# Second expert's first matrix product as seven block products, and its PReLU as a·h + |b·h|

## The chip, the cores and the metric

One core of a Trainium2 chip runs the kernel. The metric is the device time of one execution in microseconds (us); the median of three runs is compared. Engines are named as in the profile: PE (TensorE) with its weight loads PEld, DVE (VectorE), ACT (ScalarE), POOL (GpSimd), SP (which issues the transfers).

## The reference, cut to what matters

```python
X = fft(fft(x, axis=1), axis=2).real        # x: 2 x 3008 x 256, float32
x = X.reshape(6016, 256)
h = x @ w_in;  g = h / (1 + exp(-h));  x = g @ w_out          # first expert, 256 -> 2048 -> 256
h = x @ w_in2; g = max(h, 0) + alpha * min(h, 0); return g @ w_out2   # second expert (PReLU)
```

`alpha` is one number for each of the 2048 columns of `h`, between 0 and 0.3. The weights come as float64.

## The kernel before, in words

The transform uses the symmetry of real input: rows come in pairs, `NC` = 6 chunks of `CW` = 502 pairs. It runs as three short stages of matrix products (lines up to 371), the second batch's part of it beside the first expert. The first expert then has 96 rounds, one for each chunk and each of the 16 tiles `f` of 128 hidden columns; a scheduler orders these rounds and the work put beside them (`PLAN` gives the rounds), among it the conversion of the second expert's weights from float64 (`conv_w2`) and their splitting.

Everything is computed in float32r (a float32 that the writer rounds to fewer bits), with each operand as a high part and a low part: a product x·w is hi·hi + lo·hi + hi·lo, three matrix products. `split` makes the parts: ACT copies the value to float32r (high), and DVE or POOL subtracts that from the value (low).

The second expert is written out by hand, in program order (`manual_schedule`). Its 12 token tiles `t` (chunk and sign) hold 502 tokens each, transposed: 256 inputs as two blocks of 128 partitions. A round `i` is one token tile and one `f`, 192 in all:

- `h_mm`: six matrix products of 502 columns into one bank of PSUM, `ph` (lines 585 to 587: two input blocks by three products).
- `prelu_split` and `low2`: DVE takes `m` = min(ph, 0)·alpha (line 593), then max(ph, 0) + m (line 597); ACT copies to the high part `gh` (line 601); DVE subtracts for the low part `gl` (line 609).
- `mm4`, two rounds later (`LAG`): six products of 502 columns with `w_out2` into two banks, `a` (line 628), summed over the 16 `f` of a token tile. At the last `f` ACT copies both out (`ot`) and SP sends them off.

The next token tile's high and low parts (`os`) are made by `split_o1` in two pieces, ACT for the high part and POOL for the low one, at rounds 6 and 9 of the 16.

The pools that matter: `big` (ten 8 KB buffers, for inputs, raw weights, chunks `o1` and `os`), `wk` (sixteen buffers of 504 columns), PSUM `mm` (four banks, for `ph`) and `acc` (four banks, for `a`).

## Time and profile before

| | |
|---|---|
| median of 3 runs | 1012.55 us (1012.48 to 1012.71) |
| span of the profiled execution | 1009.7 us; the runs have 2.85 us around a span of that length |
| first expert's rounds | from about 36 to 477 us of the span |
| second expert's rounds | from about 471 to 1005 us |
| busy, whole span | PE 98%, PEld 80%, DVE 77%, ACT 44%, POOL 31% |

The times of matrix products are to be read with care: they are pipelined, so that the mean duration of one (about 0.39 us at 502 columns) is longer than the step from the start of one to the start of the next, and it is the step that a stream of them costs.

### The profile page before, as it was taken

Reading aid. Unit: us, or ns where it says so; the run is one execution under the profiler, and the core shown is the slowest. Engines: PE = TensorE matmul, PEld = TensorE weight load, DVE = VectorE, ACT = ScalarE, POOL = GpSimd, SP = SyncE. Lnnn points to the kernel's source line nnn. Section 1 sums busy time; section 2 is a strip of 40 time slices with the busy share of each in tenths; the row PEclk is TensorE's granted clock in tenths of the full one; section 3 lists DMA queues with packets and bytes.
Section 4 is the critical chain, followed back from the end, with each engine's and each line's share of the span. In section 5 each row is a group of like instructions: output and inputs, shape, how many; then the busy total and the mean of one; then the engine's idle time right before and its main releaser. Section 6 shows DMA issues by size and latency. Waiting matters only on the chain.

```text
span 1009.7 us, 11772 instructions
## 1 busy us (share of the span) xinstructions
PE 986.5 (98%) x4306; PEld 808.3 (80%) x4306; DVE 773.4 (77%) x1132; ACT 440.4 (44%) x776; POOL 311.0 (31%) x255
## 2 busy tenths in 40 slices
PE   7899899999999999999999999999999999999998
PEld 5677687888888788788888888888888888888886
DVE  7898799676786977978877777777767777777765
ACT  3567566564765566676422222232222223222221
POOL 3377869333355565764500000000000000000000
PEclk9799899999999999999999999999999999999999
DMA  8721100220101112000000000000000000000000
GB/s 272 242 94 43 63 22 1 63 89 1 42 1 43 57 43 84 1 18 25 0 21 1 21 1 21 1 21 20 1 21 1 21 1 21 21 0 21 1 21 21
DMA packets 16602, 36.90 MB, mean 37 GB/s; under 512 B 1824, under 2 KB 11296, under 8 KB 14880
## 3 DMA queue, kind: packets, MB, share of 16 engines
q1 hardware_dynamic: 16544, 36.15, 10.8%
q8 instruction: 34, 0.56, 0.2%
q14 instruction: 24, 0.20, 0.1%
HBM read 26.83 MB, written 9.31 MB: 36 GB/s over the span
## 4 chain that ended last, share of the span: by engine, by line
PE 88%; DVE 6%; issue 2%; DMA 1%; ACT 1%; POOL 1%; SPq 0%; DVEq 0%; ACTq 0%
PE a L628 26%; PE ph L586 9%; PE ph L587 9%; PE ph L585 9%; PE a L553 7%; PE a L555 7%; PE a L551 7%; PE pe L505 2%; PE pe L507 2%; PE pe L506 2%; PE po L505 2%; PE po L507 2%; PE po L506 2%; PE psb L318 1%; PE psa L274 1%
## 5 line engine op out<-in xcount | busy, mean ns | idle before, releaser
L601 ACT ACTIVATE gh<-m 128x502 fp32r<-128x502 f32 x192 | 120.0, 625 | 379.2 <-DVE m L597 353.6
L628 PE MATMUL a<-gh,wo 128*128 128x502 f32 x768 | 268.4, 391 | 0.0
L593 DVE TENSOR_SCALAR m<-ph,sm 128x502 f32<-128x502 f32 x192 | 142.1, 740 | 135.9 <-PE ph L587 135.4
L628 PEld LDWEIGHTS a<-gh,wo 128*128 128x128 f32 x768 | 144.6, 188 | 30.4
L533 POOL TENSOR_TENSOR gl<-t,gh 128x502 fp32r<-128x502 f32 x96 | 131.8, 1373 | 100.2 <-ACT t L521 78.8
L160 POOL TENSOR_TENSOR os<-o,os 128x502 fp32r<-128x502 f32 x24 | 29.3, 1222 | 415.8 <-ACT os L159 415.8
L609 DVE TENSOR_TENSOR gl<-m,gh 128x502 fp32r<-128x502 f32 x192 | 150.1, 782 | 1.4 <-ACT gh L601 0.4
L553 PE MATMUL a<-gl,wo 128*128 128x502 f32 x384 | 149.5, 397 | 1.1 <-POOL gl L533 1.0
L586 PE MATMUL ph<-os,wi 128*128 128x502 f32 x384 | 150.2, 391 | 0.0
L585 PE MATMUL ph<-os,wi 128*128 128x502 f32 x384 | 149.8, 390 | 0.0
L628 PE MATMUL a<-gl,wo 128*128 128x502 f32 x384 | 149.6, 390 | 0.0
L587 PE MATMUL ph<-os,wi 128*128 128x502 f32 x384 | 149.6, 389 | 0.0
L555 PE MATMUL a<-gh,wo 128*128 128x502 f32 x384 | 148.1, 394 | 0.0
L597 DVE SCALAR_TENSOR_TENSOR m<-ph,m 128x502 f32<-128x502 f32 x192 | 129.3, 673 | 0.1
L551 PE MATMUL a<-gh,wo 128*128 128x502 f32 x384 | 123.3, 396 | 5.8 <-ACT gh L520 5.8
L520 ACT ACTIVATE gh<-hp 128x502 fp32r<-128x502 f32 x96 | 59.8, 623 | 109.0 <-DVE hp L516 106.8
L513 DVE SCALAR_TENSOR_TENSOR t<-n,sm,pe 128x502 f32<-128x502 f32 x96 | 70.2, 731 | 27.3 <-PE pe L507 25.8
L551 PEld LDWEIGHTS a<-gh,wo 128*128 128x128 f32 x384 | 72.3, 191 | 22.9 <-ACT gh L520 8.3
L553 PEld LDWEIGHTS a<-gl,wo 128*128 128x128 f32 x384 | 73.3, 191 | 18.6 <-POOL gl L533 3.9
L533 POOL TENSOR_TENSOR gl<-hp,gh 128x502 fp32r<-128x502 f32 x52 | 68.5, 1318 | 60.2 <-ACT hp L521 55.1
L555 PEld LDWEIGHTS a<-gh,wo 128*128 128x128 f32 x384 | 73.2, 191 | 15.0
L587 PEld LDWEIGHTS ph<-os,wi 128*128 128x128 f32 x384 | 73.1, 190 | 15.0
(129 smaller groups left out, 1378.2 us busy)
## 6 DMA issues: line engine op xcount, KB each, us to landing
out_t<-ot SPq DMA_DIRECT2D x24, 251.0 KB, 2.5
x<-in_xs SPq DMA_DIRECT2D x8, 512.0 KB, 5.2
raw_i<-in_wi SPq DMA_DIRECT2D x8, 512.0 KB, 5.2
raw_w<-in_wi SPq DMA_DIRECT2D x4, 1024.0 KB, 5.2
raw_w<-in_wo SPq DMA_DIRECT2D x4, 1024.0 KB, 4.8
raw_o<-in_wo SPq DMA_DIRECT2D x3, 1024.0 KB, 6.5
y<-ys SPq DMA_DIRECT2D x16, 144.0 KB, 3.2
x<-in_xs SPq DMA_DIRECT2D x2, 1024.0 KB, 4.9
```

Of the source, the lines that this page charges most:

```text
L533: (nc.gpsimd if s or lo_pool(i + 1) else nc.vector).tensor_tensor(lo, h, hi.bitcast(F32), op=ALU.subtract)
L551: nc.tensor.matmul(ACC1[lb, s], hi, G[i, s][0], start=st, stop=False)
L553: nc.tensor.matmul(ACC1[lb, s], hi, G[i, s][1], start=False, stop=False)
L555: nc.tensor.matmul(ACC1[lb, s], lo, G[i, s][0], start=False, stop=sp)
L585: nc.tensor.matmul(ph, hi, OS[t][:, 2 * k, :], start=k == 0, stop=False)
L586: nc.tensor.matmul(ph, hi, OS[t][:, 2 * k + 1, :], start=False, stop=False)
L587: nc.tensor.matmul(ph, lo, OS[t][:, 2 * k, :], start=False, stop=k == 1)
L593: nc.vector.tensor_scalar(m, ph, 0.0, alpha_sb[:, f : f + 1], op0=ALU.min, op1=ALU.mult)
L597: nc.vector.scalar_tensor_tensor(m, ph, 0.0, m, op0=ALU.max, op1=ALU.add)
L601: nc.scalar.activation(hi, m, AF.Copy)
L609: nc.vector.tensor_tensor(lo, m, hi.bitcast(F32), op=ALU.subtract)
L628: nc.tensor.matmul(ACC2[lb], w[lb][j], x, start=st and first, stop=sp and last)
```

## The change: what it does

The product of the 256-row weight block with a token tile is written as a 2 by 2 block product: the two input blocks of 128 rows, and two tiles of `f` (`4g + k` and `4(g+1) + k`, so one round now holds a pair), on the weights' side; the input blocks and two halves of the tokens on the other. The halves are `L` and `R`, columns 0 to 251 and 250 to 501 (`HALF` = 252; two columns are computed twice). Eight block products become seven, on sums and differences of blocks of the weights (`prep_ws`, made once: `ws0`, `ws1`) and of the tokens (`split_o1`, made for each token tile: `xt`, then `os`). The blocks of `h` are sums of the seven products, some of which accumulate in PSUM, while others are added by DVE.

A round is now a pair of `f`: 96 rounds `n`, eight for each token tile. In a round, `outer` issues products 1 and 5 into the two halves of a bank `ac`, and ACT copies both out (`e`); `inner` issues product 2 into a bank `b`, and products 6 and 3 on top of the halves of `ac`; ACT copies the first half out (`u`); `seventh` issues product 7 on top of that half, and ACT copies it again (`u`, second half); `fourth`, in the next round, issues product 4 on top of it. DVE makes the four blocks of `h`: `h11` (`b` + `e`), `h12` (`ac` + `u`), `h22` (`u` + `e`), and the last is `ac` itself. Each of the 21 matrix products has 252 columns.

PReLU becomes a·h + |b·h|: ACT takes |b·h| (`absolute`, `q`), DVE multiplies and adds (`prelu`). The coefficients a and b come from `alpha` (`coefficients`, on POOL); their sign is moved into `w_out2`, whose rows ACT multiplies before they are split (`prep_wo2`). `mm4` is as before, six products of 502 columns for each `f`, and two rounds of pairs behind.

The new weights lie in buffers that are free by then (`WS_HOMES`), and three new ones (`xs`). `os` now takes two of the `big` buffers for each token tile.

```diff
-    "wi0": (84, 86), "wo0": (86, 87), "wi1": (88, 90), "wo1": (90, 92), "wi2": (98, 100), "wo2": (100, 102),
-    "wi3": (102, 104), "wo3": (104, 106),
+    "co": (60, 61), "ws0": (62, 80), "ws0b": (84, 92), "ws1": (80, 92), "ws1b": (93, 99),
+    "wo0": (86, 87), "wo1": (90, 91), "wo2": (97, 98), "wo3": (98, 100),
 }
+HALF = 252
+WS_ENG = "vpvpvpvpvpv" "pvpvppppppp"
...
+        A11, A12, A21, A22 = (0, 0), (0, 1), (1, 0), (1, 1)
+        steps = put_(4, *A22) + put_(1, *A11)
+        steps += form(A22, A21, A22, ALU.add) + form(A21, A11, A21, ALU.subtract)
+        steps += put_(2, *A12) + put_(5, *A22)
+        steps += form(A11, A22, A11, ALU.subtract) + put_(7, *A21)
+        steps += form(A12, A12, A11, ALU.subtract) + put_(6, *A11) + put_(3, *A12)
...
+            for q in range(2):
+                f = 4 * g + 2 * h + q
+                w = v[:, 256 * q : 256 * q + 256]
+                nc.scalar.activation(w, w, AF.Copy, scale=fc[:, 2, f : f + 1])
...
+            to, p, q = (
+                (t1, b(0, 1), b(0, 0)), (t3, b(1, 1), b(0, 1)), (t2, b(1, 1), t1), (t4, b(1, 0), t2),
+            )[n]
+            nc.gpsimd.tensor_tensor(to, p, q, op=ALU.subtract)
...
+            nc.scalar.activation(hi, src, AF.Copy)
+            nc.gpsimd.tensor_tensor(lo, src, hi.bitcast(F32), op=ALU.subtract)
...
+        for q, (w, x) in enumerate(((whi, xhi), (whi, xlo), (wlo, xhi))):
+            nc.tensor.matmul(to, w, x, start=start and q == 0, stop=q == 2, skip_group_check=True)
...
+        product(n, 1, h["ac"][:, :HALF], True)
+        product(n, 5, h["ac"][:, HALF:], False)
+        h["e"] = work(F32, f"e{n}", 2 * HALF)
+        nc.scalar.activation(h["e"], h["ac"], AF.Copy)
...
+        product(n, 2, h["b"], True)
+        product(n, 6, h["ac"][:, :HALF], False)
+        product(n, 3, h["ac"][:, HALF:], False)
...
+        nc.vector.tensor_tensor(h["h0"][:, :W], h["b"][:, :W], h["e"][:, :W], op=ALU.add)
...
+        nc.scalar.activation(h["u"][:, :HALF], h["ac"][:, :HALF], AF.Copy)
+        nc.vector.tensor_tensor(h["h0"][:, R], h["ac"][:, HALF:], h["u"][:, :HALF], op=ALU.add)
...
+        product(n, 7, h["ac"][:, :HALF], False)
+        nc.scalar.activation(h["u"][:, HALF:], h["ac"][:, :HALF], AF.Copy)
...
+        nc.vector.tensor_tensor(h["h1"][:, R], h["u"][:, HALF:], h["e"][:, HALF:], op=ALU.add)
...
+        product(n, 4, H[n]["ac"][:, :HALF], False)
...
+        nc.scalar.activation(h["q", i][:, to], source(n, part), AF.Abs, scale=coef(n, i, 1))
...
+        nc.vector.scalar_tensor_tensor(
+            h[f"h{i}"][:, to], source(n, part), coef(n, i, 0), h["q", i][:, to], op0=ALU.mult, op1=ALU.add
+        )
...
+                if t + 1 < 2 * NC and 3 <= p < 7:
+                    if p == 3:
+                        nxt = split_o1(t + 1)
+                    run(nxt[(0, 4, 6, 7)[p - 3] : (4, 6, 7, 9)[p - 3]])
...
+                if new:
+                    outer(n)
+                if old:
+                    prelu(n - 1, 0)
+                    h22(n - 1)
+                if n > 1:
+                    low2(n - 2, 1)
+                if old:
+                    absolute(n - 1, 1)
+                    high2(n - 1, 0)
+                if n < 2:
+                    mm2(n1 - LAG + n, (0,))
                 else:
-                    mm4(i - LAG)
+                    mm4(n - 2, 0)
+                if old:
+                    prelu(n - 1, 1)
+                    fourth(n - 1)
+                    absolute(n - 1, 2)
+                if new:
+                    inner(n)
+                    h11(n)
+                if old:
+                    prelu(n - 1, 2)
+                if new:
+                    h12(n)
+                if old:
+                    high2(n - 1, 1)
+                if new:
+                    absolute(n, 0)
+                if old:
+                    low2(n - 1, 0)
...
+                    mm4(n - 2, 1)
+                if new:
+                    seventh(n)
```

How this stands in the engines' queues, at three places. The first is PE in the middle of the second expert. Before, one round of one `f` (`ph` the hidden tile, `a_6_0` and `a_6_1` the two sums of a token tile):

```order
L585 MATMUL ph_6507<-os_6214,wi_1_0_4114 128x502
L586 MATMUL ph_6507<-os_6214,wi_1_0_4114 128x502
L587 MATMUL ph_6507<-os_6214,wi_1_1_4115 128x502
L585 MATMUL ph_6507<-os_6214,wi_1_2_4116 128x502
L586 MATMUL ph_6507<-os_6214,wi_1_2_4116 128x502
L587 MATMUL ph_6507<-os_6214,wi_1_3_4117 128x502
L628 MATMUL a_6_0_6479<-gh_98_6477,wo_0_0_4036 128x502
L628 MATMUL a_6_0_6479<-gl_98_6496,wo_0_0_4036 128x502
L628 MATMUL a_6_0_6479<-gh_98_6477,wo_0_1_4037 128x502
L628 MATMUL a_6_1_6480<-gh_98_6477,wo_0_0_4036 128x502
L628 MATMUL a_6_1_6480<-gl_98_6496,wo_0_0_4036 128x502
L628 MATMUL a_6_1_6480<-gh_98_6477,wo_0_1_4037 128x502
```

Now, from product 3 of a round (`ws_3h`) over the six products of `mm4` to product 7 (`ws_7h`):

```order
L671 MATMUL ac_7423<-os_0_6775,ws_3h 128x252
L671 MATMUL ac_7423<-os_1_6776,ws_3h 128x252
L671 MATMUL ac_7423<-os_0_6775,ws_3l 128x252
L769 MATMUL a_5_0_7177<-gh_44_1_7403,wo_3_0_4579 128x502
L769 MATMUL a_5_0_7177<-gl_44_1_7435,wo_3_0_4579 128x502
L769 MATMUL a_5_0_7177<-gh_44_1_7403,wo_3_1_4580 128x502
L769 MATMUL a_5_1_7178<-gh_44_1_7403,wo_3_0_4579 128x502
L769 MATMUL a_5_1_7178<-gl_44_1_7435,wo_3_0_4579 128x502
L769 MATMUL a_5_1_7178<-gh_44_1_7403,wo_3_1_4580 128x502
L671 MATMUL ac_7423<-os_0_6775,ws_7h 128x252
L671 MATMUL ac_7423<-os_1_6776,ws_7h 128x252
L671 MATMUL ac_7423<-os_0_6775,ws_7l 128x252
```

Between products that write the same bank `ac`, and that wait for ACT and DVE to have read it, stand the six products of an older `f`.

The second place is ACT in the same stretch. Before, it has one copy for each `f` (`gh2`):

```order
L601 ACTIVATE gh2_90_6311<-m90_6306 128x502
L601 ACTIVATE gh2_91_6331<-m91_6326 128x502
L601 ACTIVATE gh2_92_6351<-m92_6346 128x502
L601 ACTIVATE gh2_93_6371<-m93_6366 128x502
L601 ACTIVATE gh2_94_6391<-m94_6386 128x502
```

Now, the last part of the token tile's splitting (`os3`), and one round (the number behind a name is the round):

```order
L656 ACTIVATE os3_0_5747<-xt3_1_5681 128x504
L687 ACTIVATE e22_5888<-ac22_5881 128x504
L733 ACTIVATE q1_21_5895<-h1_21_5891,fc_86 128x252
L744 ACTIVATE gh2_21_0_5897<-h0_21_5856 128x502
L733 ACTIVATE q1_21_5895<-ac21_5816,fc_86 128x250
L705 ACTIVATE u22_5920<-ac22_5881 128x252
L744 ACTIVATE gh2_21_1_5926<-h1_21_5891 128x502
L733 ACTIVATE q0_22_5928<-h0_22_5921,fc_86 128x502
L711 ACTIVATE u22_5920<-ac22_5881 128x252
```

Two copies for a pair of `f` have become eight operations, in a fixed order in which those that PE waits for (`e`, `u`) stand behind the others.

The third place is ACT at the start of the second expert. Before (`wi2`, `wo2`: high parts of the later weights):

```order
L601 ACTIVATE gh2_2_4457<-m2_4452 128x502
L159 ACTIVATE wi2_2_2_4441<-v2_1_2666 128x512
L601 ACTIVATE gh2_3_4481<-m3_4476 128x502
L159 ACTIVATE wo2_2_0_4489<-v2_3_3715 128x512
L601 ACTIVATE gh2_4_4505<-m4_4500 128x502
L159 ACTIVATE wo2_2_0_4489<-v2_3_3715 128x512
```

Now, between the last `u` of round 0 and `e` of round 1:

```order
L711 ACTIVATE u0_4483<-ac0_4458 128x252
L513 ACTIVATE ws1_3h_4501<-v2w_1_3331 128x512
L541 ACTIVATE v2o_1_3739<-v2o_1_3739,fc_86 128x256 x2
L166 ACTIVATE wo2_2_0_4504<-v2o_1_3739 128x512
L541 ACTIVATE v2o_1_3739<-v2o_1_3739,fc_86 128x256 x2
L166 ACTIVATE wo2_2_0_4504<-v2o_1_3739 128x512
L687 ACTIVATE e1_4521<-ac1_4514 128x504
```

Seven operations on weights stand in a row there, ahead of a copy that PE's next products wait for; before, one stood between two copies.

## Rows read from the trace of the kernel before

**Rows 1.** The page: span; busy us by engine (share, instructions); last chain's shares.

```profile
span 1009.7 us, 11772 instructions
PE 986.5 (98%) x4306; PEld 808.3 (80%) x4306; DVE 773.4 (77%) x1132; ACT 440.4 (44%) x776; POOL 311.0 (31%) x255
PE 88%; DVE 6%; issue 2%; DMA 1%; ACT 1%; POOL 1%; SPq 0%; DVEq 0%; ACTq 0%
```

**Rows 2.** 780 to 1000 us: busy PE, PEld, DVE, ACT, POOL (xcount); granted clock; DMA.

```profile
780.00:1000.00 220.00, 220.00 (x965) 181.88 (x964) 161.45 (x242) 58.90 (x98) 9.38 (x8) 1.00 0.03 12
```

**Rows 3.** The page's groups: busy us, mean ns of one, idle before and releaser.

```profile
L601 ACT ACTIVATE gh<-m 128x502 fp32r<-128x502 f32 x192 | 120.0, 625 | 379.2 <-DVE m L597 353.6
L628 PE MATMUL a<-gh,wo 128*128 128x502 f32 x768 | 268.4, 391 | 0.0
L593 DVE TENSOR_SCALAR m<-ph,sm 128x502 f32<-128x502 f32 x192 | 142.1, 740 | 135.9 <-PE ph L587 135.4
```

**Rows 4.** Timeline of one round of the second expert: start us, duration us.

```profile
700.72 0.39 PE L585 MATMUL ph<-os,wi 128*128 128x502 f32 x1
...
701.87 0.40 PE L587 MATMUL ph<-os,wi 128*128 128x502 f32 x1
...
702.30 0.74 DVE L593 TENSOR_SCALAR m<-ph,sm 128x502 f32<-128x502 f32 x1 [0.83 <-PE ph L587]
...
703.46 0.38 PE L585 MATMUL ph<-os,wi 128*128 128x502 f32 x1
```

**Rows 5.** Timeline of three products of 256 columns in the first expert, with loads.

```profile
192.03 0.40 PE L274 MATMUL psa<-xr,fh 128*128 128x256 f32 x2
192.15 0.19 PEld L274 LDWEIGHTS psa<-xr,fl 128*128 128x128 f32 x1
...
192.27 0.19 PEld L505 LDWEIGHTS pe<-eo,wi 128*128 128x128 f32 x1
192.38 0.39 PE L505 MATMUL pe<-eo,wi 128*128 128x502 f32 x1
```

**Rows 6.** ACT's groups by form, from PSUM, from SBUF, and the copy out.

```profile
L156 ACT ACTIVATE ot<-a 128x502 f32<-128x502 f32 x23 | 12.2, 579 | 1.9 <-PE a L628 1.9
...
L156 ACT ACTIVATE ya<-psa 128x256 f32<-128x256 f32 x8 | 3.1, 385 | 1.7 <-PE psa L274 1.3
...
L159 ACT ACTIVATE xr<-x 128x256 fp32r<-128x256 f32 x4 | 1.4, 405 | 3.0 <-POOL xr L160 3.0
```

**Rows 7.** DVE's groups by form: half-width operations, PSUM source and SBUF sources.

```profile
L338 DVE TENSOR_TENSOR z<-psb,z 128x283 fp32r<-128x283 f32 x4 | 1.8, 455 | 5.4 <-ACT z L336 5.4
...
L252 DVE TENSOR_TENSOR x<-x 128x256 f32<-128x256 f32 x2 | 0.8, 425 | 0.1
```

**Rows 8.** POOL's groups by form: a half-width difference, and a very small copy.

```profile
L252 POOL TENSOR_TENSOR x<-x 128x256 f32<-128x256 f32 x2 | 1.5, 740 | 0.0
L254 POOL COPY slot<-x 128x4 f32<-128x4 f32 x4 | 1.6, 405 | 0.1
```

**Rows 9.** Timeline: POOL and DVE make low parts; `gl`: ns min/median/max.

```profile
537.71 0.61 ACT L159 ACTIVATE os<-o 128x502 fp32r<-128x502 f32 x1
...
538.39 1.27 POOL L160 TENSOR_TENSOR os<-o,os 128x502 fp32r<-128x502 f32 x1 [32.79 <-ACT os L159]
538.53 1.67 DVE L609 TENSOR_TENSOR gl<-m,gh 128x502 fp32r<-128x502 f32 x1
...
L609 DVE TENSOR_TENSOR gl<-m,gh x192: 670/673/1798, 479.5 to 1003.2; 128x502 fp32r<-128x502 f32 x192
```

**Rows 10.** Busy time by engine, sum over 300 to 480 us (first expert's second half).

```profile
sum 180.00, PE 177.73 PEld 144.89 DVE 139.66 ACT 113.13 POOL 108.18; mean PE 19.75 PEld 16.10 DVE 15.52 ACT 12.57 POOL 12.02
```

**Rows 11.** The transfer of `alpha` (issue, time to landing), and POOL's first low part.

```profile
31.62 0.43 SPq L700 DMA_DIRECT2D sm<-in_alpha  x1
...
40.22 1.25 POOL L533 TENSOR_TENSOR gl<-hp,gh 128x502 fp32r<-128x502 f32 x1 [0.77 <-ACT hp L521]
...
DMA to landing us min/median/max: 6.1/6.1/6.1
```

More of the change, by code (lines that the diff above doesn't have):

```diff
@@ new lines, in slab, with prep_ws, put_, high @@
+    def slab(home, name):
+        if home in ("cs", "ch"):
+            return wp.tile([128, 512], F32R, tag=home, name=name)
+        if home == "cv":
+            return cp.tile([128, 512], F32R, tag="cv", name=name)
+        if home == "xs":
+            return xp.tile([128, 512], F32R, tag="xs", name=name)
+        if home == "e128":
+            return ep.tile([128, 512], F32R, tag="e128", name=name)
+        return wp.tile([128, 512], F32R, tag=home, name=name)
+    def prep_ws(pg):
+        at = lambda i, k: V2["w", pg][:, 1024 * k + 512 * i : 1024 * k + 512 * i + 512]
+        eng = iter([nc.vector if e == "v" else nc.gpsimd for e in WS_ENG[11 * pg : 11 * pg + 11]])
+        homes = list(WS_HOMES[pg])
+        def put_(j, i, k):
+            def high():
+                hi = slab(homes.pop(0), f"ws{pg}_{j}h")
+                lo = slab(homes.pop(0), f"ws{pg}_{j}l")
+                WS[pg, j] = hi, lo
+                nc.scalar.activation(hi, at(i, k), AF.Copy)
+            def low():
+                hi, lo = WS[pg, j]
+                next(eng).tensor_tensor(lo, at(i, k), hi.bitcast(F32), op=ALU.subtract)
+            return [high, low]
+        def form(to, x, y, op):
+            return [lambda: next(eng).tensor_tensor(at(*to), at(*x), at(*y), op=op)]
+        A11, A12, A21, A22 = (0, 0), (0, 1), (1, 0), (1, 1)
[4 more added lines that the diff above has]
+        steps += form(A12, A12, A11, ALU.subtract) + put_(6, *A11) + put_(3, *A12)
+        return steps
@@ L540, in mm2 @@
         sp = f == NF - 1 or ORDER[i + 1][0] != c
-        if st:
+        if st and 0 in lbs:
             for lb in range(2):
@@ L544, in mm2 @@
                     ACC1[lb, s] = acc_ps(f"a1_{i}_{lb}{s}")
-        more = c in O1
-        if sp and not more:
+        if sp and 0 in lbs:
+            MORE[0] = c in O1
+        more = MORE[0]
+        if sp and not more and 0 in lbs:
             O1[c] = big([128, 4, CW], F32, f"o1_{c}")
-        for lb in range(2):
+        for lb in lbs:
             hi, lo = (WO[1, g, j][:, fo, lb * 128 : lb * 128 + 128] for j in range(2))
@@ L564, in mm2 @@
                         nc.scalar.activation(o, ACC1[lb, s], AF.Copy)
[L565 removed]
+        if 1 in lbs:
+            del G[i, 0], G[i, 1]
     OS = {}
     ACC2 = {}
[L571 to L588 removed]
@@ new lines, in fourth, with source, absolute @@
+    def fourth(n):
+        product(n, 4, H[n]["ac"][:, :HALF], False)
+    PART = {0: (0, slice(0, CW)), 1: (1, R), 2: (1, slice(0, W))}
+    def source(n, part):
+        i, to = PART[part]
+        return H[n]["ac"][:, :W] if part == 2 else H[n][f"h{i}"][:, to]
+    def absolute(n, part):
+        i, to = PART[part]
+        h = H[n]
+        if ("q", i) not in h:
+            h["q", i] = work(F32, f"q{i}_{n}")
+        nc.scalar.activation(h["q", i][:, to], source(n, part), AF.Abs, scale=coef(n, i, 1))
@@ new lines, in prelu, with high2, low2 @@
+    def prelu(n, part):
+        i, to = PART[part]
+        h = H[n]
+        nc.vector.scalar_tensor_tensor(
+            h[f"h{i}"][:, to], source(n, part), coef(n, i, 0), h["q", i][:, to], op0=ALU.mult, op1=ALU.add
+        )
+    def high2(n, i):
+        hi = work(F32R, f"gh2_{n}_{i}")
+        nc.scalar.activation(hi, H[n][f"h{i}"], AF.Copy)
+        G[n, i] = [hi]
+    def low2(n, i):
+        lo = work(F32R, f"gl2_{n}_{i}")
+        nc.vector.tensor_tensor(lo, H[n][f"h{i}"], G[n, i][0].bitcast(F32), op=ALU.subtract)
+        G[n, i].append(lo)
@@ L624, in mm4 @@
             order = [(lb, j, ghi) for lb in range(2) for j in range(2)] + [(lb, 0, glo) for lb in range(2)]
-        for n, (lb, j, x) in enumerate(order):
-            first = all(o[0] != lb for o in order[:n])
-            last = all(o[0] != lb for o in order[n + 1 :])
+        for m, (lb, j, x) in enumerate(order):
+            first = all(o[0] != lb for o in order[:m])
+            last = all(o[0] != lb for o in order[m + 1 :])
             nc.tensor.matmul(ACC2[lb], w[lb][j], x, start=st and first, stop=sp and last)
@@ L754, in fft_moe_kernel @@
             put(a + (b - a) * n // 8, a + (b - a) * (n + 1) // 8, steps)
+        put(*PLAN["co"], [coefficients])
+        for pg in range(2):
+            steps = prep_ws(pg)
+            put(*PLAN[f"ws{pg}"], steps[:8])
+            put(*PLAN[f"ws{pg}b"], steps[8:])
         for g in range(4):
-            put(*PLAN[f"wi{g}"], prep_wi2(g))
             put(*PLAN[f"wo{g}"], prep_wo2(g))
-        put(n1 - 5, n1 - 1, [lambda lb=lb: split_o1(0, lb) for lb in range(2)])
+        put(n1 - 5, n1 - 1, split_o1(0))
         for i in range(n1):
```

165 lines of the change are left out of this document (90 added, 75 removed).

## The prediction

> **What bounds the kernel now.** I read the page first: PE is busy 98% of the span, and 88% of the chain that ended last is PE [rows 1]. An average can hide a stage with another limit, so next came the busy time by stretch. In the second expert PE has no gap at all, 220.00 of 220.00 us at granted clock 1.00, while DVE works 161.45, ACT 58.90 and POOL 9.38 us [rows 2]. The groups say the same from the other side: ACT's copies `gh` sat idle 379.2 us, 353.6 of it until DVE's `m`, and DVE 135.4 us until the last product of `ph` [rows 3]. There the time is the count of matrix products times their step. The timeline gives that step: a round's first `ph` product starts at 700.72, the next round's at 703.46, twelve products later, so 2.74/12 = 0.228 us for 502 columns [rows 4]. A pair of `f` costs 5.48 us, and 96 pairs 526 us.
>
> **The products.** A pair goes from 24 products of 502 columns to 12 of 502 and 21 of 252. No float32r product of 252 columns is in the trace. The nearest have 256: two start from 192.03, one follows, and the next stream starts at 192.38, so a step of 0.35/3 = 0.117 us, give or take 0.003 for times shown to 0.01 us [rows 5]. In proportion to 502 columns it would be 0.1146. I take 0.116, with 0.1146 and 0.120 as bounds. A round then costs 21 x 0.116 + 12 x 0.228 = 5.18 us, 0.30 less, and 96 of them 29 us less (32 and 21 by the bounds).
>
> Each product loads its own weights, 0.19 us by the record, longer than such a step. The row says that this is latency: the loads at 192.15 and 192.27 start 0.12 us apart, under the running products [rows 5]. The Trainium skill ("TensorE: Matmul & The Clock Gate", section "Part 3: Packing small matmuls") speaks against the change here: it says that a load overlaps with products in flight only where the row groups differ, and all of these use all rows. With that page's load of 128/1.2 = 107 ns and stream of N/2.4 + 2.5 ns, an estimate is 0.21 us for a short product and 0.32 for a long one: a round of 8.3 us against 7.7 before, and the products would cost 64 us more instead of 29 less. The trace disagrees, since 0.228 leaves no room for such a load.
>
> **DVE and ACT in a round.** Half-width DVE operations cost 0.455 us at 283 columns from PSUM and 0.425 at 256 from SBUF [rows 7], so about 0.42 at 252. DVE has five of them (`h11`, `h12`, `h22`, two parts of `prelu`), one `prelu` at 502 columns (0.70, between the 0.67 of `gl` and the 0.74 of `m` [rows 3, 9]) and two low parts (0.67): 4.15 us of 5.18, about as much as before for a pair. ACT goes from two copies to eight operations: `e` 0.58, two `u` 0.385, two half `q` 0.385 and 0.405, one `q` and two high parts at 0.625 [rows 3, 6]: 4.0 us. |b·h| with a column of coefficients is priced as a copy; at most a tenth more, 0.1 us a round, still fits. So PE stays the longest by over a microsecond, if nothing waits in the wrong order.
>
> **The new waits.** Products 6, 7 and 4 write a bank that ACT and DVE have to have read. The shortest cover is that of product 7: it waits for `h12`, which waits for `u`, which waits for product 3. PE's result is ready 0.43 us after the start of a product of 502 columns, so 0.20 after its slot [rows 4]; then `u` 0.385, `h12` 0.42, and two handovers of about 0.07 (ACT's `os` ends at 538.32, POOL starts at 538.39 [rows 9]): 1.15 us. The six products of `mm4` between cover 6 x 0.228 = 1.37. The other two have about 2 us of cover for 1 to 1.3 us of work. So in an undisturbed round nothing shows, but only 0.2 us is spare at product 7, with ACT and DVE strictly in order behind it. If ACT reaches `u` late, what is late next is `h12`, product 7, and all of PE.
>
> **What disturbs the rounds.** Once in eight rounds ACT also makes the next token tile's high parts (three of 0.405, two of 0.62) and two copies out (0.58): 3.6 us against 1.1 us free in each round; two of them stand together in one round, just ahead of `e`. POOL's work in a block of eight rounds grows from two differences of 1.27 us to four forms, three half-width lows (0.74 each [rows 8]) and two lows of 504 columns: 7.7 us. POOL's work is not free for DVE: at 538.39 POOL works 1.27 us, and DVE's `gl`, begun at 538.53, takes 1.67 us, 1.0 more than the median of 0.67 and until 0.5 after POOL's end [rows 9]. Before, PE noticed nothing, as DVE had 0.8 us to spare in each round of 2.74 [rows 4]. Now DVE has 1.0 us in each of 5.18. The operations that read PSUM have one source in SBUF, so some POOL work falls beside them. I take 0.4 us lost for each of eleven such blocks, together 5 us; the bounds are 0 and 14, the latter 1.3 us a block.
>
> **The start of the second expert.** ACT now has `ws1_3h` (0.62), four scalings of 256 columns (0.405) and two splits (0.62) in a row ahead of `e` of round 1: 3.5 us [rows 3, 6]. The cover of `e` is 1.3 us up to product 6, so some 2 us reach PE; two later rounds take 1.4 us more of ACT each, and six POOL lows of 512 columns hold DVE up. I take 5 us, bounds 1 and 9. Before, one split at a time stood between two copies, and PE did not wait.
>
> **The first expert.** Added there or at its end: on POOL ten more operations of about 1.3 us, on ACT six high parts and half of the 16 scalings, on DVE four operations of 0.7 us. From 300 to 480 us POOL is busy 108 of 180 us, ACT 113, DVE 140 [rows 10], so most of it finds room. The scheduler also moves `coefficients`, planned for round 60, to just ahead of POOL's first low part. `alpha`, issued at 31.62, lands 6.1 us later, in time, but six small operations (0.25 to 0.4 us, by the 0.405 of a copy of 4 columns [rows 8]) meet 0.77 us of idle POOL [rows 11]: 1 us late. With other small shifts of the scheduler's order I take 2 us, bounds -2 and 6. At the end the work after the last `h` product is much the same: 0.
>
> **Sum.** -29 + 5 + 5 + 2 = -17 us. The profiled execution's span is 1009.7 us, 2.85 us less than the median of the runs shown; I subtract from both alike: span about 993, time 996 us.
>
> **The rivals.**
> - *The chain at product 7 binds in every round.* 0.2 us spare is little, and `u` stands behind a `q` that itself waits for product 4. For it: eight operations on ACT with five waits. Against it: 1.1 us of free ACT time in a round. At 0.15 us a round it costs 14 in place of 5: 1006 us.
> - *DVE, held by POOL, becomes the bound: slower.* Place: the rounds with the lows of `xt`, where POOL's 2.5 us meet DVE's SBUF operations. If half of POOL's 7.7 us a block reaches PE, 11 x 3.85 = 42 us are lost in place of 5: 1034 us. It decides from 0.23 us of waiting a round (22 us in all) on. Against it: 8 us of free DVE time in a block. The Trainium skill ("SBUF — State Buffer", section "SBUF: two separate sides") calls this an exclusive lock, held for the whole instruction; rows 9 agree.
> - *Loads don't hide in a long stream of short products: slower.* If each of the 21 took the 0.19 us of its load, a round would cost 6.7 us and the kernel 1012.6 + 120 = 1132 us. The row with three such products shows no sign, but it is only three. The skill's rule on loads, above, is the same mechanism.
> - *No loss at all.* Only the products count: 1012.6 - 29 to 32, so 981 to 984 us.
> - *It doesn't do what it says* in time: waits of 0.23 us a round give back all: 1012 us.
>
> **How the numbers follow.** Forecast with its small losses (987 to 1003 us) 0.55; no loss 0.11; chain at product 7 (1003 to 1010) 0.13; all given back 0.06; DVE held by POOL 0.11; loads 0.04. The likeliest is 996 us, its own range 987 to 1003. From 983 to 1013 us I leave out the two slower cases, 0.15, and a part of the best one, 0.05. A measurement of this kernel can tell about 0.2%, 2 us: faster 0.79, same 0.06, slower 0.15.
>
> **What would show it.** Steps of 0.116 us within a run of short products, with loads as far apart; rounds of 5.2 us between the starts of product 1; PE's idle time in the second expert below 15 us, and what there is before products 6 or 7, in one or two rounds of eight and in the first four; ACT and DVE each near 80% busy; low parts of 1.5 us and more wherever POOL works. I am wrong if the steps are 0.15 us or more, if PE waits in every round, or if the first expert's rounds have moved by more than 6 us.

## The result, and the profile after

The changed kernel takes 994.09 us (median of 991.82, 993.93, 994.25 and 994.53), the kernel before 1012.51 us beside it: a ratio of 0.9817, 95% interval 0.9803 to 0.9831. The profiled execution took 993.93 us with a span of 992.2 us, 17.5 us less than the 1009.7 of [rows 1].

The page after (span; busy us by engine; shares of the chain that ended last; four groups, to be read as [rows 3]):

```profile
span 992.2 us, 14364 instructions
...
PE 961.0 (97%) x5170; PEld 826.1 (83%) x5170; DVE 789.3 (80%) x1328; ACT 711.2 (72%) x1410; POOL 405.3 (41%) x355
...
PE 79%; DVE 8%; issue 4%; ACT 3%; POOL 3%; DMA 2%; SPq 0%; ACTq 0%; DVEq 0%; POOLq 0%
...
L738 DVE SCALAR_TENSOR_TENSOR h<-h,fc,q 128x502 f32<-128x502 f32 x192 | 130.3, 678 | 38.8 <-ACT q L733 36.7
...
L749 DVE TENSOR_TENSOR gl<-h,gh 128x502 fp32r<-128x502 f32 x192 | 140.6, 732 | 0.1
...
L744 ACT ACTIVATE gh<-h 128x502 fp32r<-128x502 f32 x192 | 118.4, 617 | 2.1 <-DVE h L738 2.1
...
L705 ACT ACTIVATE u<-ac 128x252 f32<-128x252 f32 x96 | 36.6, 381 | 51.7 <-PE ac L671 51.7
```

PE still stands on nearly all of the span. ACT is no longer the idle engine that [rows 3] showed (`gh` had 379.2 us of idle time ahead of it): in the second expert its largest idle time is now 51.7 us, that of the 96 copies `u`, which wait for product 3.

The same views by stretch: the middle of the second expert (answers to [rows 2]), and the first expert's second half (answers to [rows 10]):

```profile
680.00:960.00 280.00, 280.00 (x1785) 254.09 (x1785) 225.32 (x434) 228.54 (x479) 58.03 (x56) 1.00 0.04 14
...
300.00:480.00 180.00, 174.39 (x765) 141.91 (x764) 139.05 (x196) 119.61 (x216) 125.12 (x101) 0.99 0.09 32
```

In the second expert PE again has no gap, now with DVE and ACT busy 80% and 82%. The first expert is where PE stands still more than before: 5.6 us of 180 in place of 2.3.

The timeline of one round (start, duration; answers to [rows 4, 5]):

```profile
700.75 0.42 DVE L706 TENSOR_TENSOR h<-ac,u 128x252 f32<-128x252 f32 x1 [0.30 <-ACT u L705]
...
701.28 0.41 PEld L671 LDWEIGHTS ac<-os,ws_7h 128*128 128x128 f32 x2
...
701.50 0.40 PE L671 MATMUL ac<-os,ws_7h 128*128 128x252 f32 x2
701.62 0.19 PEld L671 LDWEIGHTS ac<-os,ws_7l 128*128 128x128 f32 x1
701.73 0.27 PE L671 MATMUL ac<-os,ws_7l 128*128 128x252 f32 x1
...
702.54 0.39 PE L769 MATMUL a<-gh,wo 128*128 128x502 f32 x1
...
706.66 0.40 PE L671 MATMUL ac<-os,ws_7h 128*128 128x252 f32 x2
```

Nine short products run from 701.50 to 702.54, a step of 0.116 us, with each load under the products ahead of it. The round from product 7 to product 7 is 5.16 us here; over the nine groups of eight rounds that lie wholly in the steady part it is 41.4 to 41.6 us, so 5.18 a round, against 16 x 2.74 = 43.84 for the same work before [rows 4].

Set side by side, the two traces put the 17.5 us as follows. Twelve groups of eight rounds at 43.84 - 41.45 = 2.39 us make -28.7. From the first to the last matrix product that starts in the second expert it is 533.9 us before and 509.5 after, -24.4: so 4.3 us were given back in this stage, outside the steady rounds. Its first product starts 6.8 us later than before, counted from the first matrix product of each kernel. And -28.7 + 4.3 + 6.8 = -17.6.

### The profile page after: what moved, and what is told of

It is laid out like the page before. It is cut to its first block, busy times and chain, and to the rows that moved or that the text cites. A ratio compares the mean times of both kernels' runs of the same rounds, so it can differ in the third digit from the quotient of the medians.

```text
span 992.2 us, 14364 instructions
## 1 busy us (share of the span) xinstructions
PE 961.0 (97%) x5170; PEld 826.1 (83%) x5170; DVE 789.3 (80%) x1328; ACT 711.2 (72%) x1410; POOL 405.3 (41%) x355
## 4 chain that ended last, share of the span: by engine, by line
PE 79%; DVE 8%; issue 4%; ACT 3%; POOL 3%; DMA 2%; SPq 0%; ACTq 0%; DVEq 0%; POOLq 0%
PE a L769 26%; PE ac L671 20%; PE a L611 6%; PE a L613 6%; PE a L609 6%; PE b L671 3%; PE pe L561 2%; PE po L561 1%; PE pe L563 1%; PE pe L562 1%; PE po L563 1%; PE po L562 1%; PE psb L326 1%; DVE hp L572 1%; ACT gh L576 1%
## 5 line engine op out<-in xcount | busy, mean ns | idle before, releaser
L738 DVE SCALAR_TENSOR_TENSOR h<-h,fc,q 128x502 f32<-128x502 f32 x192 | 130.3, 678 | 38.8 <-ACT q L733 36.7
L749 DVE TENSOR_TENSOR gl<-h,gh 128x502 fp32r<-128x502 f32 x192 | 140.6, 732 | 0.1
L744 ACT ACTIVATE gh<-h 128x502 fp32r<-128x502 f32 x192 | 118.4, 617 | 2.1 <-DVE h L738 2.1
L733 ACT ACTIVATE q<-h,fc 128x502 f32<-128x502 f32 x192 | 116.9, 609 | 3.0 <-DVE h L716 1.4
L647 POOL TENSOR_TENSOR xt<-o 128x252 f32<-128x252 f32 x24 | 17.1, 732 | 187.1 <-ACT q L733 149.7
L611 PEld LDWEIGHTS a<-gl,wo 128*128 128x128 f32 x384 | 73.7, 192 | 20.1 <-POOL gl L589 4.5
L572 DVE TENSOR_TENSOR hp<-t,po 128x502 f32<-128x502 f32 x96 | 64.5, 672 | 20.2 <-PE po L563 16.6
L769 PEld LDWEIGHTS a<-gl,wo 128*128 128x128 f32 x384 | 72.4, 189 | 7.5
L705 ACT ACTIVATE u<-ac 128x252 f32<-128x252 f32 x96 | 36.6, 381 | 51.7 <-PE ac L671 51.7
L657 POOL TENSOR_TENSOR os<-o,os 128x252 fp32r<-128x252 f32 x36 | 32.8, 924 | 92.6 <-ACT os L656 92.6
```

The costliest lines, as they stand in the source:

```text
L572: nc.vector.tensor_tensor(hp, t, po, op=ALU.add)
L611: nc.tensor.matmul(ACC1[lb, s], hi, G[i, s][1], start=False, stop=False)
L733: nc.scalar.activation(h["q", i][:, to], source(n, part), AF.Abs, scale=coef(n, i, 1))
L738: nc.vector.scalar_tensor_tensor(h[f"h{i}"][:, to], source(n, part), coef(n, i, 0), h["q", i][:, to], op0=ALU.mult, op1=ALU.add)
L744: nc.scalar.activation(hi, H[n][f"h{i}"], AF.Copy)
L749: nc.vector.tensor_tensor(lo, H[n][f"h{i}"], G[n, i][0].bitcast(F32), op=ALU.subtract)
```

## The experiments

All are edits of the changed kernel. My theory was that the second expert's time is the number of product columns, that the losses sit in the first expert (the new weights' work on POOL and DVE) and at the start of the second (ACT's weight work ahead of `e`), and that the disturbed rounds of the steady part cost nothing. The rivals: the steady rounds are set by the chain at product 7, by DVE, or by POOL.

**One product more.**

```diff
         product(n, 7, h["ac"][:, :HALF], False)
+        product(n, 7, h["ac"][:, :HALF], False)
```

> Product 7 is issued twice in each of the 96 rounds (so h holds it twice), which makes eight block products of 252 columns again. My theory, that the second expert's time is the count of product columns and nothing else: 3 products of 0.116 us more in a round, 0.35 us, 33 us in all, 1027 us, with rounds of 5.53 us and no wait on PE. Rival, that ACT, DVE or a chain of waits sets the round and the gain came from elsewhere: the three products fall into free time, 994 to 1005 us. Rival, that loads hide only in short runs: more than 45 us.

1024.42 us (1022.84 to 1026.01), ratio to the kernel before 1.0121 (1.0082 to 1.0160). Eight rounds take 44.2 us, 2.75 more, or 0.1146 us for each of the 24 products, and PE has no gap. The columns are the price, and eight products by halves, with all else as in the change, would have made the kernel slower than it was: the one product in eight that is saved is worth more than the whole gain. The median moved by 30.3 us, and the profiled execution by 28.9, not 33: the second expert takes 31.7 us more from its first to its last product, since the wait for `e` at the start is partly covered by the product added, and the first expert of this execution ended 2.9 us earlier.

**Less cover for product 7.** The last product, or the last three, of the second `mm4` of a round go behind it (k = 5 or 3):

```diff
...
-                    mm4(n - 2, 1)
+                    mm4(n - 2, 1, (0, k))
                 if new:
                     seventh(n)
+                if n > 1:
+                    mm4(n - 2, 1, (k, 6))
```

> The last product of the second mm4 of a round goes behind product 7, so that five products of 502 columns cover the chain from product 3 to product 7 in place of six: 0.228 us less cover. In the changed kernel product 7 starts 0.286 us after h12's end in the median, and 0.055 us where PE waited for it, so 0.23 us is spare. My theory: the spare time is just used up, 0 to 0.03 us a round, 0 to 4 us in all, 994 to 998 us. Rival, that the cover has much to spare: no change here, and none in the run with three covering products. Rival, that the chain binds already wherever POOL or ACT disturb a round: 5 to 20 us.

> Three of the six products of the second mm4 go behind product 7: 0.684 us less cover, 0.23 us of it spare. My theory: PE waits 0.46 us for h12 in every round, 44 us in all, 1038 us, and the round is 5.64 us; the waits stand ahead of product 7 and nowhere else. Rival, that the engines' order has slack and product 7 is not on a tight chain: 994 us. Rival, that the delay is passed round to the next round's products too: over 60 us.

With five covering products: 1007.67 us (1006.37 to 1010.48), ratio 0.9972 (0.9954 to 0.9990), so 13.6 more than the changed kernel and not 0 to 4; that lies in the range of the rival by which the chain binds where POOL or ACT disturb a round. With three: 1047.00 us (1045.39 to 1048.60), ratio 1.0344 (1.0305 to 1.0383), 53 more and not 44. Both are dearer than I had worked out from the spare time, and the timeline of the run with three says why:

```profile
701.10 0.42 DVE L706 TENSOR_TENSOR h<-ac,u 128x252 f32<-128x252 f32 x1 [0.36 <-ACT u L705]
...
701.57 0.30 PEld L671 LDWEIGHTS ac<-os,ws_7h 128*128 128x128 f32 x2 [0.73 <-DVE h L706]
701.57 0.49 PE L671 MATMUL ac<-os,ws_7h 128*128 128x252 f32 x2 [0.32 <-DVE h L706]
701.79 0.19 PEld L671 LDWEIGHTS ac<-os,ws_7l 128*128 128x128 f32 x1
701.90 0.27 PE L671 MATMUL ac<-os,ws_7l 128*128 128x252 f32 x1
```

What waits for `h12` is the load of product 7, not the product alone. It starts 0.05 us after `h12` ends, and the first two products of the block then stand 0.221 us apart in the median (0.116 in the changed kernel, where the load starts 0.22 ahead of its product). So a wait costs its length and 0.105 us more for a load that nothing hides. The spare time at product 7 is therefore not the 0.23 us from `h12`'s end to the product's slot that I had read, but 0.23 - 0.105 = 0.12. That gives 0.56 us a round with three covering products; the median round is 5.73, 0.55 more. With five it gives 0.11, and the median round is 5.28, 0.10 more. More than half of the loss is one round in eight, in which POOL makes the low parts of `xt`: it takes 6.0 us, 0.8 more, of the 1.4 that eight rounds lose. Its timeline in the run with five:

```profile
642.34 2.98 POOL L657 TENSOR_TENSOR os<-xt,os 128x504 fp32r<-128x504 f32 x2 [4.51 <-ACT os L656]
642.43 1.75 DVE L749 TENSOR_TENSOR gl<-h,gh 128x502 fp32r<-128x502 f32 x1
...
644.10 1.50 DVE L738 SCALAR_TENSOR_TENSOR h<-h,fc,q 128x252 f32<-128x252 f32 x1
...
646.23 0.41 DVE L706 TENSOR_TENSOR h<-ac,u 128x252 f32<-128x252 f32 x1
...
646.69 0.50 PE L671 MATMUL ac<-os,ws_7h 128*128 128x252 f32 x2 [0.51 <-DVE h L706]
```

Two operations of DVE are held up by 2.1 us together while POOL works, `h12` is late, and PE waits. In the changed kernel the same round meets POOL otherwise (the longest `gl` there is 1.22 us) and loses nothing; that no operation came at a worse moment is luck. The rival "the chain at product 7" was thus close: 0.12 us of cover less a round and it would have begun.

**PReLU as it was.** DVE takes min(h, 0)·alpha and max(h, 0) plus that:

```diff
...
-        nc.scalar.activation(h["q", i][:, to], source(n, part), AF.Abs, scale=coef(n, i, 1))
+        nc.vector.tensor_scalar(h["q", i][:, to], source(n, part), 0.0, alpha_of(n, i), op0=ALU.min, op1=ALU.mult)
...
-            h[f"h{i}"][:, to], source(n, part), coef(n, i, 0), h["q", i][:, to], op0=ALU.mult, op1=ALU.add
+            h[f"h{i}"][:, to], source(n, part), 0.0, h["q", i][:, to], op0=ALU.max, op1=ALU.add
```

> Seven products as in the change, but PReLU as it was: DVE takes min(h, 0) times alpha and then max(h, 0) plus that, and ACT takes no absolute value. DVE gets three more operations in a round, 0.74 + 0.45 + 0.45 = 1.6 us, on 4.2 us of now; ACT loses 1.7 us. My theory: DVE becomes the bound, rounds of 5.85 us in place of 5.18, 64 us more, 1058 us, with PE idle in every round until DVE. Rival, that PE stays the bound because part of DVE's work was waiting for ACT: 994 to 1000 us, and then the new PReLU buys nothing.

1018.06 us (1017.66 to 1019.14), ratio 1.0067 (1.0044 to 1.0090): 24 us more, neither 64 nor none. The median round is 5.24 from product 1 to product 1, hardly longer. Eight rounds take 43.5 us, 2.05 more, most of it in one wait of product 7 for `h12` in each token tile, up to 1.4 us long. Why eleven operations fit is in DVE's timeline of a quiet round:

```profile
707.61 0.68 DVE L754 TENSOR_TENSOR gl<-h,gh 128x502 fp32r<-128x502 f32 x1
708.20 0.68 DVE L743 SCALAR_TENSOR_TENSOR h<-h,q 128x502 f32<-128x502 f32 x1
708.79 0.41 DVE L721 TENSOR_TENSOR h<-u,e 128x252 f32<-128x252 f32 x1
709.12 0.67 DVE L754 TENSOR_TENSOR gl<-h,gh 128x502 fp32r<-128x502 f32 x1
709.71 0.34 DVE L738 TENSOR_SCALAR q<-h,sm 128x252 f32<-128x252 f32 x1
```

Each starts about 0.08 us before the one ahead of it has ended by its record: 0.59 us apart for operations of 0.68, 0.33 for one of 0.41. A sum of durations overstates what DVE needs by 0.08 us an operation. And min(h, 0)·alpha from one tile in SBUF costs less than the 0.74 and 0.45 that I had set: 0.48 at 502 columns, 0.34 at 252. The new PReLU carries more than the whole gain all the same: without it seven products are slower than the kernel before.

**More work on POOL.** Two, or four, subtractions of 252 columns at the head of every round, on a tile of their own (`dm`; k = 2 or 4):

```diff
...
+                for _ in range(k):
+                    nc.gpsimd.tensor_tensor(dm, dm, dm, op=ALU.subtract)
```

> Two subtractions of 252 columns on POOL, on a tile that nobody else uses, are added at the head of every round of the second expert: 2 x 0.73 = 1.46 us of POOL work a round beside its own 7.7 us in eight rounds. DVE has 4.2 us of work in 5.18, 3.0 of it on operations with all operands in SBUF. Theory of the prediction (POOL holds up DVE's SBUF operations, and DVE's 1.0 us of free time takes what it can): 0 to 20 us more, 994 to 1014, with low parts of over 1 us in most rounds. If POOL and DVE work beside each other undisturbed: 994 us, low parts at 0.67. If POOL's time is all lost to DVE: 0.48 us a round, 46 us more, 1040 us.

> Four such subtractions a round, 2.9 us of POOL work: with its own work POOL is busy 3.9 of 5.18 us. If POOL and DVE take turns for operations in SBUF, DVE's 3.0 us and POOL's 2.9 us do not fit into 5.18: 5.9 us a round at least, 69 us more (1063 us), and at most 4.2 + 2.9 = 7.1 us, 185 us more. If they work beside each other: 994 us. Between the two (they slow each other by a part): 1000 to 1060 us.

With two: 996.64 us (996.26 to 997.02), ratio 0.9855 (0.9837 to 0.9873), eight rounds 41.6 us, PE without a gap. With four: 1011.45 us (1010.45 to 1014.12), ratio 1.0005 (0.9994 to 1.0015), eight rounds 43.0. The busy times of the run with four (columns as in [rows 2]), and its DVE groups:

```profile
680.00:900.00 220.00, 216.39 (x1351) 189.43 (x1351) 204.11 (x328) 169.47 (x364) 172.78 (x211) 1.00 0.04 13
```

```profile
L749 DVE TENSOR_TENSOR gl<-h,gh 128x502 fp32r<-128x502 f32 x82 | 75.5, 920 | 0.0
L738 DVE SCALAR_TENSOR_TENSOR h<-h,fc,q 128x252 f32<-128x252 f32 x41 | 36.8, 898 | 0.0
L716 DVE TENSOR_TENSOR h<-u,e 128x252 f32<-128x252 f32 x41 | 31.3, 762 | 2.7 <-ACT u L711 2.7
...
L706 DVE TENSOR_TENSOR h<-ac,u 128x252 f32<-128x252 f32 x41 | 16.6, 404 | 0.0
```

Most of DVE's operations with all operands in SBUF are stretched in the mean (`gl` 0.92 for 0.67, `h22` 0.76 for 0.42, the `prelu` of 252 columns 0.90 for 0.48; the one of 502 columns, 0.74, is not), those that read PSUM are not (`h12` 0.40). So POOL does take time from DVE, and free time of DVE pays for it first: two operations are absorbed, four bring the kernel back to the time before the change. The Trainium skill ("SBUF — State Buffer", section "SBUF: two separate sides") calls the shared port a lock held for the whole instruction. Single rows agree; the sum does not quite: at their undisturbed pace DVE's operations in SBUF need 2.57 us a round and POOL's about 3.7, 6.3 together in a round of 5.38. A part of each instruction lies beside the other engine's; which part no run here shows.

**The weight scalings earlier, and the coefficients later.** The sixteen scalings become steps of rounds 78 to 95, and the last splits are spread over four rounds; in another run the coefficients stand behind POOL's low part of round 57 (`lo`):

```diff
...
-                nc.scalar.activation(w, w, AF.Copy, scale=fc[:, 2, f : f + 1])
...
-    "wo0": (86, 87), "wo1": (90, 91), "wo2": (97, 98), "wo3": (98, 100),
+    "wo0": (86, 87), "wo1": (90, 91), "wo2": (97, 99), "wo3": (99, 101), "sc0": (78, 86), "sc1": (88, 96),
...
+            put(*PLAN[f"sc{g}"], [lambda f=f: scale_wo2(f) for f in range(8 * g, 8 * g + 8)])
```

```diff
...
-        put(*PLAN["co"], [coefficients])
+        put(*PLAN["co"], [lambda: behind(coefficients, ("lo", 57))])
```

> The sixteen scalings of the second output weights become steps of their own in the first expert's rounds 78 to 95 instead of standing ahead of their splits, and the splits of the last two groups are spread over rounds 97 to 100. ACT then has four splits and one or two high parts of weights in the second expert's first rounds, but no scalings. Theory: the 1.6 us wait of product 6 for e in the second round goes, and the 0.7 us in the first may stay: 1.5 to 2.5 us less between the first product of the second expert and the end; the first expert is put in another order by the scheduler, which moves its end by -3 to +3 us. Rival, that the start's loss is the first expert's unfinished work (silu, mm2) and not the weights: no change there.

> The six small operations that make the coefficients are held behind POOL's low part of round 57 of the first expert; in the changed kernel the scheduler puts them ahead of POOL's first low part. Theory: the 0.8 us by which rounds 5 to 50 of the first expert run behind the kernel before go to 0; what follows round 57 is put in another order, which may give back or add 3 us at the end of the first expert: 990 to 996 us. Rival, that the 0.8 us comes from other shifts of the scheduler's order at rounds 2 to 4: rounds 5 to 50 stay 0.8 us behind.

Early scalings: 990.67 us (989.18 to 992.93), ratio 0.9805 (0.9791 to 0.9818). The second expert from its first to its last product takes 505.3 us in place of 509.5: the 4.2 us are nearly the whole loss of that stage (4.3), twice what I had expected, and more than the scatter: the two other runs that leave the scalings and PE's products as they were take 508.2 and 508.9 us. The largest single wait in the changed kernel stands in these rows at its start, 1.9 us with the load that it delays; 0.8 come before it, at `e` of round 0, and 1.5 behind it, up to round 4:

```profile
487.60 0.63 ACT L166 ACTIVATE wo<-v2o 128x512 fp32r<-128x512 f32 x1
...
488.14 0.89 ACT L541 ACTIVATE v2o<-v2o,fc 128x256 f32<-128x256 f32 x2
...
489.06 0.63 ACT L166 ACTIVATE wo<-v2o 128x512 fp32r<-128x512 f32 x1
489.60 0.57 ACT L687 ACTIVATE e<-ac 128x504 f32<-128x504 f32 x1
...
490.22 0.50 PE L671 MATMUL ac<-os,ws_6h 128*128 128x252 f32 x2 [1.61 <-ACT e L687]
```

Late coefficients: 990.70 us (989.62 to 992.75), ratio 0.9798 (0.9785 to 0.9812). At round 20 this run is 1.0 us behind the kernel before; the run with early scalings, whose coefficients still stand at the front, is 1.2 ahead there, and six others with the instructions of the changed kernel up to that point lie between 1.8 ahead and 3.0 behind. So the theory fails, as the 0.8 us did not go, but the rival's reason, the scheduler's order, is not shown either: a scatter of 4.9 us between executions hides any effect of this size. The medians of both runs are 3.4 us below that of the changed kernel, but the intervals of the ratios overlap with its own.

**The weights' sums and low parts paced, or left out.** From here on the first expert is read in one way: how far the products `pe` of a round have fallen behind the kernel before, beyond what they were at round 54. In one run, made on top of the early scalings, the 22 operations are held behind their planned rounds; in the other, made on the changed kernel, they are left out, and products use high parts twice and blocks of the weights as they are:

```diff
...
+            steps = [lambda st=st: paced(st) for st in steps]
...
+        def paced(st):
+            i = LAST["now"]
+            if i < n1:
+                behind(st, ("t", i - 1), ("lo", i - 2))
```

```diff
...
-                WS[pg, j] = hi, lo
+                WS[pg, j] = hi, hi
...
-            return [high, low]
+            return [high]
...
+        form = lambda *a: []
```

> The early scalings of the run before, and in addition the sums and low parts of the new weights are held behind the first expert's round for which they are planned (DVE's behind t of the round before, POOL's behind the low part of two rounds before), so that the scheduler no longer draws the first eight of them together into rounds 54 to 58. Read as the distance that the first expert's rounds fall behind the kernel before from round 54 to its end, which was 5.1 to 6.5 us in the changed kernel and six like it, and 7.6 with the early scalings. Theory, that these operations cost because several stand ahead of hp in one round: 2 to 4 us, and 986 to 989 us in all. Rival, that their sum on DVE and POOL costs wherever it stands: 5 to 7.5 us, 990 to 991 us.

> The changed kernel without the eight sums and fourteen low parts of the new weights (products use the high part twice, and blocks of the weights as they are): it takes 8 operations of 0.7 us from DVE and 14 of 1.3 us from POOL, and nothing else. Theory, that this work is what sets the first expert back: from round 54 to the end it falls behind the kernel before by 0 to 2 us in place of 5.1 to 6.5, and the time is 987 to 990 us. Rival, that the conversions' new places and the scheduler's order do it: 4 to 6.5 us, 993 to 994 us.

Paced: 989.67 us (988.50 to 990.79), ratio 0.9788 (0.9774 to 0.9802). Left out: 987.95 us (986.18 to 990.11), ratio 0.9770 (0.9752 to 0.9788). The distances, in us, each the difference of two traces' start times ("end" is the first product of the second expert):

| run | round 57 | round 80 | round 84 | round 94 | end |
|---|---|---|---|---|---|
| changed kernel | 1.5 | 2.2 | 5.3 | 6.3 | 6.3 |
| six runs with the same first expert | 1.5 to 1.6 | 2.2 to 2.3 | 4.6 to 5.6 | 5.8 to 7.1 | 5.1 to 6.4 |
| early scalings | 1.6 | 2.3 | 4.6 | 7.6 | 7.6 |
| late coefficients | 1.6 | 0.8 | 3.7 | 5.2 | 5.2 |
| all paced | 0.1 | 1.9 | 2.1 | 2.5 | 4.9 |
| left out | 0.6 | 1.4 | 1.6 | 1.5 | 1.5 |
| ws0 paced | 0.1 | 1.9 | 5.8 | 5.8 | 10.6 |
| ws0 paced, sums early | 0.1 | 3.8 | 6.1 | 6.7 | 9.0 |

Without these operations 4.8 of the 6.3 us are gone, so they are the main cost in the first expert. Pacing moves it: nothing is lost at round 57 (where the changed kernel makes up 1.1 of its 1.5 us by the next round) and little at 84, but 2.4 us in the last two rounds, and the second expert takes 508.2 us again. The 4.9 us at the end lie between the ranges of theory and rival, and the time is not clear of that of the run with early scalings alone (990.67, intervals overlap): that pacing gains anything in all is not shown. What one such place looks like, around round 82 of the changed kernel (`v2w`: sums for the weights, `ws_2l`: a low part, L187 and L191: conversion):

```profile
406.64 1.75 DVE L522 TENSOR_TENSOR v2w<-v2w 128x512 f32<-128x512 f32 x1 [1.81 <-POOL v2w L522]
...
409.55 1.92 DVE L187 TENSOR_SCALAR v2o<-raw_w 128x512 uint32<-128x512 uint32 x2
...
411.15 1.46 POOL L517 TENSOR_TENSOR ws_2l<-v2w,ws_2h 128x512 fp32r<-128x512 f32 x1
...
411.39 1.77 DVE L191 SCALAR_TENSOR_TENSOR v2o<-raw_w,v2o 128x512 uint32<-128x512 uint32 x1
...
413.08 0.67 DVE L572 TENSOR_TENSOR hp<-t,po 128x502 f32<-128x502 f32 x1
...
413.84 0.62 ACT L576 ACTIVATE gh<-hp 128x502 fp32r<-128x502 f32 x1 [3.49 <-DVE hp L572]
...
414.52 0.71 PE L609 MATMUL a<-gh,wo 128*128 128x502 f32 x2 [1.83 <-ACT gh L576]
```

POOL's work makes DVE's conversions long (L191 takes 0.68 us undisturbed, 1.77 here), `hp` stands behind them in DVE's order, `gh` waits 3.49 us for it and PE 1.83.

**Two tries at a better place.** Both with the early scalings: only ws0 paced; and with it two of the four sums of each half made earlier:

```diff
...
-            steps = [lambda st=st: paced(st) for st in steps]
+            steps = [lambda st=st: paced(st) for st in steps] if pg == 0 else steps
```

```diff
...
-        steps += put_(2, *A12) + put_(5, *A22)
-        steps += form(A11, A22, A11, ALU.subtract) + put_(7, *A21)
-        steps += form(A12, A12, A11, ALU.subtract) + put_(6, *A11) + put_(3, *A12)
+        steps += put_(2, *A12) + form(A11, A22, A11, ALU.subtract) + form(A12, A12, A11, ALU.subtract)
+        steps += put_(5, *A22) + put_(7, *A21) + put_(6, *A11) + put_(3, *A12)
```

> As the paced run, but only the first half's sums and low parts (ws0) are held behind their rounds; those of the second half (ws1) come where the scheduler puts them, since in the paced run they were pushed into the last rounds of the first expert and the first of the second. Theory, that the place decides (one operation at a time in rounds with free DVE time costs nothing, several near the end do): from round 54 to the end 3 to 4 us behind in place of 4.9, and a start of the second expert as in the run with early scalings (505.3 us from its first to its last product, in place of 508.2): 986 to 988 us. Rival, that the sum of the work is paid wherever it stands: 4.9 to 7.6 us there, and 989 to 991 us in all.

> As the run with ws0 paced, and two more of the four sums of each half, which need no new buffer, are made with the first lows instead of among the last ones, so that four operations leave the crowded rounds 84 to 99. Theory, that the crowded rounds are what is left: 0.5 to 2 us less than the run with ws0 paced, 985 to 988 us. Rival, that the sum of the work is paid wherever it stands: the same as that run within its interval.

991.94 us (991.55 to 997.46), ratio 0.9819 (0.9799 to 0.9839), and 992.33 us (991.23 to 994.06), ratio 0.9815 (0.9801 to 0.9828). Neither theory is borne out. The first comes above the ranges of theory and rival; the second takes the same as the first, as its rival has it. The traces lose 10.6 and 9.0 us in the first expert, but that of the first is of its slowest execution (997.46 us, at a mean granted clock of 0.980 against 0.986 to 0.989 in the other four), so its 10.6 us hold more than the edit. That the work is paid wherever it stands is nearer than that its place decides, but it does not say how much. Each of these edits, leaving the work out included, also puts the scheduler's other work in a new order, and I can't tell the two apart; this stays open. The fastest version that computes the reference is the one with all paced and the scalings early, 989.67 us; its interval (up to 0.9802) and that of the changed kernel (from 0.9803) just do not meet.

## Why the prediction came out: step by step

- **Products, -29 us: right, also in its terms.** Steps of 0.116, rounds of 5.18, -28.7. The rival that loads don't hide is out: 0.116 us a product, with a load of 0.19 for each.
- **Disturbed rounds, +5 us: too dear; it was 0.** Eight rounds take 41.4 to 41.6 us, what the products alone need. The step that failed is "DVE has 1.0 us in each of 5.18", a sum of durations. By starts (0.08 us less than the duration for each), DVE's eight operations of a round need 4.3 - 8 x 0.08 = 3.6 us, so that 1.5 us were free, and POOL's hold (some 11 us in all over 21 of the 192 low parts, none over 1.22 us long, and some 10 us over a third of the `prelu` operations of 252 columns) went into that; DVE still idles 1.0 us a round. The rows of before held the sign of it: DVE idles 0.83 us in a round of 2.74 [rows 4], so its three operations take 1.91 us, and not the 2.08 of their durations (0.74, 0.67 for the low part [rows 9], and 0.67 here):

```profile
700.80 0.67 DVE L597 SCALAR_TENSOR_TENSOR m<-ph,m 128x502 f32<-128x502 f32 x1
```

  For before I had read the idle time, for after I summed durations. The run with the old PReLU and those with more POOL work show this room and where it ends. The Trainium skill ("Perfetto Trace Analysis", section "Optimizing Scalar/DVE Operations") has the rule that I missed: half of an instruction's recorded overhead overlaps with the next one. The trace bears out the overlap, 0.08 us; that it is half of the overhead no run here shows. I had expected low parts of 1.5 us and more wherever POOL works; in the changed kernel none is that long.
- **The chain at product 7: right in its order, and tighter than I put it.** "Only 0.2 us is spare" is 0.12, since the load needs 0.105 us of it. In the changed kernel that was enough in all but one round behind the fourth (round 11, 0.16 us), which is also luck in where POOL's lows fall.
- **ACT in a round: too cheap, without effect.** |b·h| does not cost "at most a tenth more" than a copy: `q` takes 0.72, 0.50 and 0.47 us in place of 0.625, 0.385 and 0.405, so 0.27 us more a round, and ACT had the room.
- **Start of the second expert, +5: right, 4.3**, and by the mechanism named: at `e` of round 1, where I had "some 2 us", it is 1.9. The 0.8 us at `e` of round 0 I had not named. With the scalings moved and the splits spread the whole is 0.1.
- **First expert, +2: mis-sized, 6.8**, above its bound of 6 and above the 6 us at which I said that I would be wrong. In the seven traces with this first expert it is 3.8 to 8.3; the part behind round 54, 5.1 to 6.4, is the firm one. "So most of it finds room" failed: busy shares of 60 to 78% do not say whether an operation on DVE or POOL stands ahead of `hp`. Leaving the weights' sums and lows out takes away 4.8 us. The 1 us for `coefficients` can't be told from the scatter.
- **Tail, 0: right.** From the last product's start to the span's end 4.9 us before and 5.0 after.
- **Time beside the span.** I added 2.85 us; the executions after lie 1.7 to 1.8 above their spans. A span forecast of 993 against 992.2 is thus closer than 996 against 994.09.

The sum was right by luck: a term that was too dear by 5 and one that was too cheap by 4.8 met. As to the rival of DVE held by POOL: it took some 2.8 us more POOL work in each round to bring back the time before the change, as the run with four subtractions shows.

## What to carry to other kernels

Where PE has no gap, columns saved are time saved, as long as the engines that take over the additions keep free time in the same rounds: here that took moving the absolute value to ACT. Read an engine's need from the starts of operations that follow one another, not from the sum of durations, and a product's slot from its load. Work put into a stage that is not yet bound is not free: ask what stands behind it in its engine's order.

## What I had not expected of the hardware

- A product whose load had to wait loses 0.105 us beyond the wait: the first two products of 252 columns stand 0.221 us apart in place of 0.116.
- DVE's records overlap by 0.08 us from one operation to the next, so that eleven operations with durations of 5.4 us together fit a round of 5.21, with 0.4 us of idle time left in it.
- After PE's two waits of 1.83 and 0.83 us around 415 us the granted clock of the changed kernel is 0.51 from 416.87 to 420.28 us, the lower of its two levels, 1.2 GHz:

```profile
416.39 0.39 PE L562 MATMUL po<-eo,wi 128*128 128x502 f32 x1
...
417.28 0.62 PE L613 MATMUL a<-gh,wo 128*128 128x502 f32 x1
417.70 0.62 PE L611 MATMUL a<-gl,wo 128*128 128x502 f32 x1
...
420.69 0.39 PE L561 MATMUL pe<-eo,wi 128*128 128x502 f32 x1
```

  Steps of 0.42 us stand between steps of 0.23. Four other executions with the same two waits (1.7 to 2.0 and 0.8 us), of the runs with one product more, three covering products, the old PReLU and four POOL operations, kept 1.00 from 400 to 425 us. At round 84 they were 4.6 to 5.0 us behind, those with the lower clock 5.2 to 5.6. This may be one source of the 2.7 us between the fastest and the slowest execution of the changed kernel, whose mean granted clocks are 0.989 and 0.984; only one of its executions has a trace.
- The same instructions reach round 54 of the first expert between 2.1 us ahead of and 2.8 behind the kernel before, a scatter as large as several of the terms that were to be told apart.
